# An adaLN transformer block on one core: first MLP weights are split during the first attention block, and the plan counts the queue of transfers

## The chip, the cores and the metric

One core of a Trainium2 chip runs the whole program. The metric is device time in microseconds of one execution; lower is better.

## The reference

One block of a transformer with adaptive layer norm: 2048 rows of 576, 32 heads of 18, an MLP of width 4608, all in float32.

```python
mod = (_silu(c) @ w_mod).reshape(c.shape[0], 6, 1, -1)
sa, ca, ga, sb, cb, gb = (mod[:, i] for i in range(6))
h = layernorm(x) * (1 + ca) + sa
x = x + ga * (softmax(q @ k.T * Dh**-0.5) @ v) @ wo     # q, k, v = h @ wqkv, by head
h = layernorm(x) * (1 + cb) + sb
x = x + gb * (silu(h @ w1) @ w2)
```

## The kernel before

**Blocks.** After a start that makes the keys, values and the first queries, the rows are worked on in four blocks of 512 (`NQB`). A block's attention goes in eight groups of four heads. An *attention step* is one `psa` matmul (scores by query, of which VectorE takes row maxima, `mx`, L966) and one `psb` matmul (scores by key, of which ScalarE takes the exponential, `pt`, L1049); a group has 64 of them, the `psa` stream runs 38 pairs of steps ahead (`LEAD`), and the products with the values (`psv`, L1057) follow. A group's row maxima go through a transpose (`pst`), a copy (`mt`, L990) and a small transfer into the rows of the query tile (`qt<-mt`, L995); the group's first `psb` waits for that transfer.

**What fills TensorE beside attention.** Beside the first block's attention stand the projections that are left (their weights `wqkv` are loaded raw, L768, and split by ScalarE, L773, and GpSimd, L778). Beside a later block's attention stands everything after attention of the block before (`post`): output projection with `wo`, layer norm, and the MLP in 18 pairs of first-layer tiles (`mlp1`) and nine groups of four second-layer tiles (`mlp2`; group i needs four tiles `w2t` of 128x576). The last block's MLP stands alone at the end.

**Weights.** A float32 product is made of three products of rounded parts, so every weight tile is split into a high part and a low part. On first use, beside the second block's attention, each half of a tile of `wo`, `w1` and `w2` is loaded raw (L1104, three buffers `raw`), scaled by a gate on GpSimd for `wo` and `w2` alone (L1107), split by GpSimd (L1110 a cast, L1113 a subtraction), and the finished tile is stored (L1116). Later blocks load the split tile whole (`wload`, the branch for `b` over 0).

**The order.** All engines run in an order that a planner writes. It keeps a time for TensorE and four other queues (ScalarE, VectorE, GpSimd, SP), and a beam search chooses at each point between an attention step, values, and the next item of the fill. SP issues every DMA, in the order in which the planner sees its operations become ready. In the plan a transfer has landed a fixed time after its issue, whatever else is under way:

```python
LAND, LANDW = 2300, 4000
    def issue(self, dur, key, at=0):
        self.push((Op(SP_, dur, self.real and self.real.load(key), (("k", key),), LAND),), 0, max(self.t + 500, at))
```

and an engine takes what became ready first (`heappop`). A half of a weight tile waits in the plan for the half before it to be issued and for the half three places before it to be split.

Of the kernel before, what the change touches and what calls it, by code (L numbers as in the profile page):

```python
# [68 lines left out]
LAND, LANDW = 2300, 4000  # L69
# [24 lines left out]
class Op:  # L94


    __slots__ = ("eng", "dur", "emit", "sets", "lag")

    def __init__(self, eng, dur, emit=None, sets=(), lag=0):
        self.eng, self.dur, self.emit, self.sets, self.lag = eng, dur, emit, sets, lag  # L100
# [11 lines left out]
class Sim:  # L112


    def __init__(self, fill, ends, loads):
# [3 lines left out]
        self.t = self.n = self.w = 0  # L119
# [62 lines left out]

    def set(self, sets, now, lag=0):
        end = now + lag
        for x in sets:
# [115 lines left out]
    def slots(self):  # L301
# [40 lines left out]
        if j == 0:  # L342
            q = sa // 32 + 1
            if q < NQB * NQUAD and sa == load_at(q):
                self.issue(1440, ("Q", q), late)
            n = sa // 8 + 1
            if sa % 8 == 0 and 6 <= n < 4 * NQB * NQUAD:
                self.issue(1280, ("ka", n))
            n = sb // 8 + 1
            if sb % 8 == 0 and n < 4 * NQB * NQUAD:  # L350
                self.issue(1280, ("kb", n))
            if w == 16 and i + 1 < NQB * NQUAD:
                self.issue(400, ("V", i + 1))
# [12 lines left out]
    def issue(self, dur, key, at=0):  # L366

        self.push((Op(SP_, dur, self.real and self.real.load(key), (("k", key),), LAND),), 0, max(self.t + 500, at))
# [35 lines left out]
    def rows(self):  # L404
# [10 lines left out]
        if kind == "m":  # L415
            self.work(110, "full", rel)
            e = self.real.max_b(i) if self.real else (None, None)
            self.push((Op(DVE_, 270, e[0], (slot,)), Op(SP_, ROWS, e[1], (("k", ("mr", i)),), LAND)), 0, self.t + 150)
# [226 lines left out]
def tile_adaln_block(ctx: ExitStack, tc: tile.TileContext, x, wqkv, wo, w1, w2, c, wfirst, wcol, out):  # L645
# [192 lines left out]
    def add_qk(steps, add):  # L838
        def load(i):
# [12 lines left out]
            add(Item(0, lambda: None, chains=((0, (Op(SP_, 10 if i == 1 else 500, begin, (), 0 if i == 1 else 3000), Op(ACT_, 740, hi), Op(GPS_, 1620, lo, (("k", ("w", i)),)))),)))  # L852

        n_mod = 0
        for i, (which, m, pairs) in enumerate(steps):
            for ns in pairs:
# [12 lines left out]
                def ends(box, which=which, m=m, ns=ns, pid=pid, names=names):  # L869
                    for g in range(2):  # L870
# [8 lines left out]
                        def store(g=g, hl=hl):  # L879
# [3 lines left out]
                               Op(SP_, 1800 if which == XM else 900, store, (("k", names[g]),), LAND))  # L883
# [22 lines left out]
    mods = [(m, t) for m in range(2) for t in range(KT)]  # L906
    FILL.append(Item(0, lambda: None, chains=((0, (Op(DVE_, 280, lambda: mod_load(*mods[0]), (("k", ("dg", mods[0])),)),)),)))
# [171 lines left out]

    def open_mlp():  # L1080
# [10 lines left out]
    def weights(make, src, scr, key, gate=None):  # L1091

        box, sets = {}, []
        for half in range(2):
# [23 lines left out]
            chain = [Op(SP_, 430, load, [], LAND)]  # L1118
            if gate is not None:
                chain.append(Op(GPS_, 804, scaled))  # L1120
            chain += [Op(GPS_, 445, high), Op(GPS_, 880, low, [])]
            if half:
                chain[-1].sets.append(("k", key))
                chain.append(Op(SP_, 390, store))
# [12 lines left out]
    def wload(make, src, scr, key, b, gate=None):  # L1137

        if b == 0:
            return (), tuple(weights(make, src, scr, key, gate))  # L1140
        return ((300, (Op(SP_, 390, lambda: nc.sync.dma_start(f(make()), f(scr)), (("k", key),), LANDW),)),), ()
# [6 lines left out]
    def x_op(b, j):  # L1148
        return Op(SP_, 400, lambda: x_load(b, j), (("k", ("x1", b, j)),), LAND)
# [31 lines left out]
    def post(b, add):  # L1181
# [188 lines left out]
        def mlp2(i0, put):  # L1370
            for j in range(NST):
# [16 lines left out]
                after = (Op(SP_, 400, store, (), LAND),) + ((x_op(b + 1, j + 1),) if b + 1 < NQB and j + 1 < NST else ())  # L1388
# [48 lines left out]
    OPEN.fn, OPEN.keys = open_mlp, tuple(sorted(made))  # L1437
# [451 lines left out]
```

## Time and profile before

| | |
|---|---|
| median of 3 runs | 2495.27 us (2494.88 to 2499.73) |
| the profiled execution | 2495.22 us, span 2493.4 us |
| block ends (last copy into `ot`) | 611.6, 1179.5, 1705.5, 2223.2 us |
| TensorE busy, mean granted clock | 2393.6 us, 0.986 |

The page has a busy time for each engine, 40 slices of the span in tenths, the DMA queues, the chain of work that ended last, and the costliest groups of instructions. In a table of windows the columns are the busy time of each engine with its count of instructions, then the granted TensorE clock, the DMA share (mean of 16 DMA engines) and GB/s. In a list of waits the numbers are the total in us, how often, and the longest. In a timeline they are start and duration in us, and in brackets how long the engine sat idle before and what released it. In a list for one tile they are the shortest, median and longest duration in ns, and the first and last start in us. PE is TensorE, DVE VectorE, ACT ScalarE, POOL GpSimd; SPq is the queue of SyncE.

### The profile page before, as it was taken

What the parts mean: (1) busy time and instruction counts of PE and PEld (TensorE: products, weight loads), DVE (VectorE), ACT (ScalarE), POOL (GpSimd) and SP (SyncE); (2) the same over time, 40 slices, a digit from 0 to 9 for tenths busy, and PEclk for the clock granted to TensorE, in tenths of its full rate; (3) what the DMA queues carried; (4) which work ended last, traced back from release to release, by engine and by line L of the source; (5) the groups of instructions that cost most, each with busy time, mean ns of one, the idle gap of its engine ahead of it and who ended that gap; (6) DMA issues with size and microseconds to landing.
All of it is one profiled execution on the core that took longest, in us unless ns stands there. A gap on an engine that the chain in (4) does not pass through costs nothing.

```text
span 2493.4 us, 52598 instructions
## 1 busy us (share of the span) xinstructions
PE 2393.6 (96%) x20528; PEld 1646.3 (66%) x20528; DVE 1784.4 (72%) x3180; ACT 1498.3 (60%) x2712; POOL 578.1 (23%) x729
## 2 busy tenths in 40 slices
PE   5999999998999999989999999999999999999999
PEld 4874545443566666665666667766677667678988
DVE  7877787787867777767877777778877778424333
ACT  5246776665656666656666776666776677652121
POOL 4100000003455565555121111111311111110000
PEclk9999999998999999999999999999999999999999
DMA  7744434435456565556455544544545555426463
GB/s 248 255 154 153 142 110 140 148 115 180 150 182 203 189 208 188 184 188 224 142 170 184 195 151 149 186 147 160 191 155 168 173 180 172 138 105 241 172 219 120
DMA packets 190711, 428.68 MB, mean 172 GB/s; under 512 B 21442, under 2 KB 58722, under 8 KB 190466
## 3 DMA queue, kind: packets, MB, share of 16 engines
q1 hardware_dynamic: 190466, 425.33, 51.0%
q8 instruction: 164, 2.69, 0.5%
q14 instruction: 81, 0.66, 0.1%
HBM read 338.92 MB, written 85.80 MB: 170 GB/s over the span
## 4 chain that ended last, share of the span: by engine, by line
PE 83%; DMA 6%; DVE 4%; POOL 4%; ACT 1%; issue 1%; SPq 1%; ACTq 0%; POOLq 0%; DVEq 0%
PE ps L722 26%; PE psv L1057 17%; PE psa L964 12%; PE ps L716 10%; PE psb L1047 9%; PE psqk L722 3%; DMA raw<-in_w 2%; PE psp L722 2%; DVE mx L966 2%; PE psv L722 2%; DMA raw<-in_wqkv 1%; DMA kt<-kscr 1%; POOL w2t L1113 1%; POOL raw L1107 1%; PE psv L1617 1%
## 5 line engine op out<-in xcount | busy, mean ns | idle before, releaser
L966 DVE TENSOR_REDUCE mx<-psa 128x1 f32<-128x512 f32 x2048 | 1347.3, 687 | 406.8 <-PE psb L1047 197.5
L1049 ACT ACTIVATE pt<-psb 128x512 f32<-128x512 f32 x2048 | 1169.9, 597 | 597.7 <-PE psb L1047 337.2
L1047 PE MATMUL psb<-qt,kt 56*128 56x512 f32 x2048 | 814.6, 428 | 20.8 <-ACT pt L1049 13.8
L964 PE MATMUL psa<-kt,qt 54*128 54x512 f32 x2048 | 769.1, 416 | 11.1 <-DVE mx L966 8.2
L964 PEld LDWEIGHTS psa<-kt,qt 54*128 54x128 f32 x2048 | 362.7, 187 | 235.4 <-DVE mx L966 128.2
L1057 PE MATMUL psv<-pt,vt 128*32 128x512 f32 x4096 | 507.6, 606 | 0.1
L722 PE MATMUL ps<-w2t,g 64*128 64x288 f32 x4992 | 445.7, 301 | 25.2 <-POOL w2t L1110 14.2
L722 PEld LDWEIGHTS ps<-w2t,g 64*128 64x128 f32 x4992 | 396.1, 189 | 100.9 <-issue 43.1
L1047 PEld LDWEIGHTS psb<-qt,kt 56*128 56x128 f32 x2048 | 365.5, 186 | 78.7 <-ACT pt L1049 62.4
L722 PE MATMUL ps<-hh,w1t 64*128 64x512 f32 x2160 | 383.6, 398 | 0.4 <-POOL w1t L1113 0.3
L722 PEld LDWEIGHTS ps<-hh,w1t 64*128 64x128 f32 x2160 | 213.0, 186 | 57.4 <-ACTq L729 12.3
L1355 POOL TENSOR_TENSOR g<-etmp,g 128x512 fp32r<-128x512 f32 x108 | 137.9, 1292 | 451.4 <-ACT g L1351 436.1
L1057 PEld LDWEIGHTS psv<-pt,vt 128*32 128x32 f32 x4096 | 103.8, 109 | 209.7 <-issue 201.1
L1217 POOL TENSOR_TENSOR x<-x,gt 128x288 f32<-128x288 f32 x116 | 92.9, 801 | 542.3 <-ACT gt L1213 530.6
L722 PE MATMUL ps<-hl,w1t 64*128 64x512 f32 x864 | 178.3, 392 | 0.0
L1210 DVE TENSOR_TENSOR x<-ps,x 128x288 f32<-128x288 f32 x184 | 83.7, 455 | 102.1 <-PE ps L716 70.6
L716 PE MATMUL ps<-w2t,g 128*128 128x288 f32 x960 | 130.1, 295 | 1.4 <-ACT g L1351 0.9
L716 PEld LDWEIGHTS ps<-w2t,g 128*128 128x128 f32 x960 | 128.6, 188 | 2.8 <-ACT g L1351 1.2
L1344 ACT ACTIVATE eq<-ps 128x512 f32<-128x512 f32 x36 | 21.5, 598 | 146.4 <-PE ps L716 146.4
L716 PE MATMUL ps<-hh,w1t 128*128 128x512 f32 x360 | 106.9, 390 | 0.5 <-DVE hh L696 0.5
L778 POOL TENSOR_TENSOR wql<-raw,wqh 128x640 fp32r<-128x640 f32 x13 | 20.8, 1599 | 371.1 <-ACT wqh L773 303.4
L722 PEld LDWEIGHTS ps<-hl,w1t 64*128 64x128 f32 x864 | 88.7, 186 | 14.9
(134 smaller groups left out, 2138.5 us busy)
## 6 DMA issues: line engine op xcount, KB each, us to landing
kt<-kscr SPq DMA_DIRECT2D x1024, 108.0 KB
w1t<-w1s SPq DMA_DIRECT2D x108, 640.0 KB
w2t<-w2s SPq DMA_DIRECT2D x108, 576.0 KB
w1s<-w1t SPq DMA_DIRECT2D x36, 640.0 KB
w2s<-w2t SPq DMA_DIRECT2D x36, 576.0 KB
vt<-vscr SPq DMA_DIRECT2D x32, 608.0 KB
qt<-qscr SPq DMA_DIRECT2D x128, 108.0 KB
raw<-in_w SPq DMA_DIRECT2D x72, 160.0 KB
```

The lines of the kernel that those rows point to most:

```text
L716: mm(self.ps[late], lhsT=lhsT, rhs=rhs, start=(i == 0), stop=(i == self.n - 1))
L722: done = mm(self.ps[g], lhsT=lhsT[rows], rhs=rhs[rows], start=(s == 0), stop=(s == 2 * self.n - 1))
L964: mm(ps, lhsT=t["q"][64 * j:64 * j + 54, hp, stt * P:(stt + 1) * P], rhs=t["k", kc, hp][64 * j:64 * j + 54, :], start=True, stop=True)
L966: return lambda: nc.vector.tensor_reduce(t["mx"][:, 2 * j + hp, stt, kc:kc + 1], ps, axis=AX.X, op=ALU.max)
L1047: mm(ps, lhsT=t["kb", kt // 4, hp][64 * e:64 * e + 56, kt % 4 * P:(kt % 4 + 1) * P], rhs=t["q"][64 * e:64 * e + 56, hp, :], start=True, st ...
L1049: return lambda: nc.scalar.activation(t["P"][kt, hp][:, e, :], ps, AF.Exp, scale=SCALE)
L1057: mm(t["ps"][32 * h:32 * h + 32, :], lhsT=t["v"][:, c0:c0 + 32], rhs=t["P"][kt, h // 2][:, h % 2, :], start=(kt == 0), stop=(kt == NKT - 1 ...
L1107: nc.gpsimd.tensor_tensor(d["raw"], d["raw"], gate[:, d["cs"]], op=ALU.mult)
L1113: nc.gpsimd.tensor_tensor(box["w"][:, 0, d["cs"]], d["raw"], f(box["w"][:, 1, d["cs"]]), op=ALU.subtract)
L1210: nc.vector.tensor_add(c["x1", j][:, hs], ps, c["x1", j][:, hs])
L1217: nc.gpsimd.tensor_add(c["x1", j][:, HH:], c["x1", j][:, HH:], box.pop("gt"))
L1355: (nc.vector if last else nc.gpsimd).tensor_tensor(gt[:, 1, :], d["t"], f(gt[:, 0, :]), op=ALU.subtract)
```

## The change

**The first MLP weights.** A new item (`SPLIT`) stands at the very start of the fill of the first block. It runs two chains, for the even and the odd halves of the 36 tiles of `w1`. Each has one raw buffer and one output buffer, and goes round: SP stores the half that this chain split last and loads its next one, GpSimd casts, GpSimd subtracts. When the last halves are stored, two keys are set, for which the opening of the MLP's buffers at the end of the first block now waits too. Beside the second block's attention the tiles of `w1` are then loaded whole, as in the later blocks; `w2` and `wo` are split there as before.

**The plan.** In place of the fixed landing times each transfer has a length in the queue (`MOVE`); transfers follow each other in one queue, and a result is seen some time after. An SP operation with a transfer that follows another operation of its chain, or that waits for a join, is pushed back by `SLACK`, 2500 ns. GpSimd takes, of the operations that are ready, those first that are not marked `late`; the weight splits are.

```diff
-LAND, LANDW = 2300, 4000
+FIRST, SEEN, SLACK = 1000, 500, 2500
+MOVE = {"k": 4 * 608, "q": 4 * 608, "v": 2300, "m": 320, "raw": 645, "w": 1700, "ws": 1480, "x": 780, "qk": 1640, "rawqk": 1280}
...
     def pop(self, e, s):
-        _, _, chain, i = heappop(self.queue[e])
+        q = self.queue[e]
+        if e == GPS_ and len(q) > 1:
+            x = min((x for x in q if x[0] <= s), key=lambda x: (x[2][x[3]].late, x[0], x[1]))
+            q.remove(x)
+            heapify(q)
+            _, _, chain, i = x
+        else:
+            _, _, chain, i = heappop(q)
...
         end += TR
+        land = end
+        if e == SP_ and op.data:
+            land = self.dma = max(min(s + 330, end) + FIRST, self.dma) + op.data
+            land = max(land, end + FIRST) + SEEN
         if op.sets:
-            self.set(op.sets, end, op.lag)
+            self.set(op.sets, end, land)
         if i + 1 < len(chain):
-            self.push(chain, i + 1, end + op.lag)
+            self.push(chain, i + 1, land + (SLACK if chain[i + 1].eng == SP_ and chain[i + 1].data > MOVE["m"] else 0))
...
                 if n + 1 == x[2]:
-                    self.push(x[3], 0, self.keys[x[1]][1])
+                    self.push(x[3], 0, self.keys[x[1]][1] + (SLACK if x[3][0].eng == SP_ else 0))
...
+    def split(n):
+        d = {}
+        def load(k):
+            d["raw"] = wqp.tile([P, 320], F32, name=f"w1raw{n}", bufs=1)
+            nc.sync.dma_start(d["raw"], w1[k // 2][:, k % 2 * 320:k % 2 * 320 + 320])
+        def store(k):
+            nc.sync.dma_start(f(w1s[k // 2][:, :, k % 2 * 320:k % 2 * 320 + 320]), f(d["out"]))
+        def high():
+            d["out"] = wqp.tile([P, 2, 320], F32R, name=f"w1out{n}", bufs=1)
+            nc.gpsimd.tensor_copy(d["out"][:, 1], d["raw"])
+        def low():
+            nc.gpsimd.tensor_tensor(d["out"][:, 0], d["raw"], f(d["out"][:, 1]), op=ALU.subtract)
+        def turn(k):
+            if k >= 2:
+                store(k - 2)
+            if k < 2 * NFT:
+                load(k)
+        chain = []
+        for k in range(n, 2 * NFT, 2):
+            chain += [Op(SP_, 400 if k < 2 else 800, lambda k=k: turn(k), (), MOVE["raw"] if k < 2 else MOVE["raw"] + 740), Op(GPS_, 445, high, late=True), Op(GPS_, 880, low, late=True)]
+        chain.append(Op(SP_, 400, lambda: turn(2 * NFT + n), (("k", ("w1s", n)),), 740))
+        return tuple(chain)
...
-            chain = [Op(SP_, 430, load, [], LAND)]
+            chain = [Op(SP_, 430, load, [], MOVE["raw"])]
...
-        if b == 0:
+        if b == 0 and gate is not None:
             return (), tuple(weights(make, src, scr, key, gate))
...
-    OPEN.fn, OPEN.keys = open_mlp, tuple(sorted(made))
+    SPLIT.chains = (0, split(0)), (4000, split(1))
+    OPEN.fn, OPEN.keys = open_mlp, tuple(sorted(made)) + (("w1s", 0), ("w1s", 1))
```

**Where instructions moved.** SP's queue in the first block, around the row maxima of the third group of heads; before, only keys (`kt`), values and projection tensors stand there:

```order
L948 DMA kt_79<-kscr 54x512 x2
L948 DMA kt_80<-kscr 54x512 x2
L948 DMA kt_81<-kscr 54x512 x2
L948 DMA kt_82<-kscr 54x512 x2
L995 DMA qt<-mt 2x8x128 x2
L948 DMA kt_83<-kscr 54x512 x2
L948 DMA kt_84<-kscr 54x512 x2
```

The same place after the change, where `w1raw` is a raw half and `w1out` a split one:

```order
L962 DMA kt_81<-kscr 54x512 x2
L962 DMA kt_82<-kscr 54x512 x2
L1103 DMA w1s<-w1out_3394 256x1x320
L1100 DMA w1raw_3440<-in_w 128x320
L1009 DMA qt<-mt 2x8x128 x2
L1103 DMA w1s<-w1out_3437 256x1x320
L1100 DMA w1raw_3490<-in_w 128x320
L962 DMA kt_83<-kscr 54x512 x2
L962 DMA kt_84<-kscr 54x512 x2
L1103 DMA w1s<-w1out_3492 256x1x320
L1100 DMA w1raw_3553<-in_w 128x320
```

A store and a load of a half stand between nearly every two chunks of keys, some ten such turns in a group; the 72nd store stands in the eighth group. The first load of a half stands far ahead, in the start, and its two GpSimd operations stand between the first power and the first copy (L1546) of the start's layer norm.

SP's queue at the end of the first block, around the row maxima of the second block's first group, before; `raw<-in_wo` is half a tile of `wo`, `wos` the store of a split one:

```order
L1104 DMA raw<-in_wo 128x288 x2
L948 DMA kt_81<-kscr 54x512 x2
L948 DMA kt_82<-kscr 54x512 x2
L1104 DMA raw<-in_wo 128x288
L1116 DMA wos<-wo_6973 256x1x576
L995 DMA qt<-mt 2x8x128 x2
L1104 DMA raw<-in_wo 128x288
```

and after:

```order
L1148 DMA raw<-in_wo 128x288
L962 DMA kt_81<-kscr 54x512 x2
L962 DMA kt_82<-kscr 54x512 x2
L1148 DMA raw<-in_wo 128x288
L1009 DMA qt<-mt 2x8x128 x2
L1148 DMA raw<-in_wo 128x288
L1160 DMA wos<-wo_7422 256x1x576
L1148 DMA raw<-in_wo 128x288
```

The maxima stood behind seven loads and two stores of `wo` and stand behind three loads and no store now.

TensorE's queue in the second block, at the end of a group's second first-layer pair (`ps<-hh,w1t`) and the start of its second-layer product (`ps<-w2t,g`), before:

```order
L722 MATMUL ps_14633<-hh,w1t 128x512
L722 MATMUL ps_14634<-hh,w1t 128x512
L722 MATMUL ps_14633<-hh,w1t 128x512
L722 MATMUL ps_14634<-hh,w1t 128x512
L1057 MATMUL psv_14786<-pt_2083,vt_2094 32x512 x2
L1057 MATMUL psv_14786<-pt_2084,vt_2094 32x512 x2
L1057 MATMUL psv_14786<-pt_2085,vt_2094 32x512 x2
L1057 MATMUL psv_14786<-pt_2086,vt_2094 32x512 x2
L1064 MATMUL pso<-ident,ov 128x128 x4
L722 MATMUL ps_14819<-w2t,g 128x288
```

and after:

```order
L1061 MATMUL psb<-qt,kt_83 128x512
L978 MATMUL psa<-kt_77,qt 128x512
L1061 MATMUL psb<-qt,kt_84 128x512
L734 MATMUL ps_15024<-hh,w1t 128x512
L734 MATMUL ps_15025<-hh,w1t 128x512
L734 MATMUL ps_15024<-hh,w1t 128x512
L734 MATMUL ps_15025<-hh,w1t 128x512
L978 MATMUL psa<-kt_77,qt 128x512
L1061 MATMUL psb<-qt,kt_84 128x512
L1071 MATMUL psv_14551<-pt_2087,vt_2094 32x512 x2
L1071 MATMUL psv_14551<-pt_2088,vt_2094 32x512 x2
L734 MATMUL ps_15324<-w2t,g 128x288
```

More attention stands there now. From the first matmul of the group's second first-layer pair to the first with `w2t`, the first eight groups of the second block hold 14, 13, 13, 12, 12, 14, 13 and 10 attention steps before, 101 in all, and 16, 15, 21, 16, 12, 22, 23 and 25 after, 150 in all. In the second half of the fourth block's attention these products stand at the same attention steps as before.

More of the change, by code (lines that the diff above doesn't have):

```diff
@@ L1 @@
-from heapq import heappop, heappush
+from heapq import heapify, heappop, heappush
 from contextlib import ExitStack
@@ L364, in slots, with issue @@
         return True
-    def issue(self, dur, key, at=0):
-        self.push((Op(SP_, dur, self.real and self.real.load(key), (("k", key),), LAND),), 0, max(self.t + 500, at))
+    def issue(self, dur, key, what, at=0):
+        self.push((Op(SP_, dur, self.real and self.real.load(key), (("k", key),), MOVE[what]),), 0, max(self.t + 500, at))
     def values(self, n):
@@ L882, in ends @@
                         yield (Op(ACT_, 600, hi), Op(DVE_, 690, lo, (("p", pid, g),)),
[L883 removed]
+                               Op(SP_, 1800 if which == XM else 900, store, (("k", names[g]),), MOVE["qk"]))
                 out = pair_items(lambda it: None, pid, make, GR, MMC, 14, lambda g, i=i: [("w", i)] if i and g[0] == 0 else [], ends)
@@ L1386, in store @@
                     nc.sync.dma_start(out[b * QB + j * P:b * QB + (j + 1) * P, :], c["x1", j])
-                after = (Op(SP_, 400, store, (), LAND),) + ((x_op(b + 1, j + 1),) if b + 1 < NQB and j + 1 < NST else ())
+                after = (Op(SP_, 400, store, (), MOVE["x"]),) + ((x_op(b + 1, j + 1),) if b + 1 < NQB and j + 1 < NST else ())
                 join = (("j", ("out", b, j), 2, after),) if i0 + CH == NFT else ()
```

36 lines of the change are left out of this document (19 added, 17 removed).

## Prediction

> **What bounds the kernel now.** I read the page first, then the busy times block by block, then who TensorE waits for, then the stretches around those waits.
>
> ```profile
> span 2493.4 us, 52598 instructions
> PE 2393.6 (96%) x20528; PEld 1646.3 (66%) x20528; DVE 1784.4 (72%) x3180; ACT 1498.3 (60%) x2712; POOL 578.1 (23%) x729
> PE   5999999998999999989999999999999999999999
> POOL 4100000003455565555121111111311111110000
> PEclk9999999998999999999999999999999999999999
> ```
>
> TensorE is 96% busy, so only its gaps and its clock are to be had. GpSimd works hard in slices 9 to 19 alone. The four blocks of rows end where GpSimd copies a block's last attention columns (`ot`):
>
> ```profile
> L1078 POOL COPY ot<-ot x4: 396/396/397, 611.6 to 2223.2; 128x256 f32<-128x256 f32 x4
> 1179.48 0.40 POOL L1078 COPY ot<-ot 128x256 f32<-128x256 f32 x1
> 1705.48 0.40 POOL L1078 COPY ot<-ot 128x256 f32<-128x256 f32 x1 [0.20 <-DVE ot L1075]
> core 0: us, PE busy (x) PEld busy (x) DVE busy (x) ACT busy (x) POOL busy (x), PEclk, DMA share, GB/s
> 220.50:611.60 391.10, 368.44 (x2369) 179.84 (x2367) 303.14 (x539) 262.59 (x485) 28.54 (x36) 0.96 0.44 142
> 611.60:1179.50 567.90, 535.09 (x4899) 361.11 (x4900) 424.45 (x720) 363.06 (x656) 321.44 (x447) 0.97 0.58 188
> 1179.50:1705.50 526.00, 523.24 (x5086) 360.11 (x5084) 410.76 (x721) 363.31 (x659) 88.21 (x92) 1.00 0.50 169
> ```
>
> So the second block takes 567.9 us and the third, with the same kinds of work and 187 more matmuls, 526.0: 41.9 us more. The waits in the second block and one of them in time (SP, then GpSimd, then TensorE) say why:
>
> ```profile
> PE ps L722 <- POOL w2t L1110: 14.2, 7, 5.0
> PE ps L722 <- POOL w2t L1113: 10.5, 10, 2.7
> PE psT L1259 <- DVE ot L1245: 2.6, 1, 2.6
> 1060.70 0.36 SPq L1104 DMA_DIRECT2D raw<-in_w  x1
> 1066.47 0.79 POOL L1107 TENSOR_TENSOR raw<-raw,gb 128x288 f32<-128x288 f32 x1 [5.31 <-DMA raw<-in_w]
> 1067.80 0.61 PE L722 MATMUL ps<-w2t,g 64*128 64x288 f32 x2 [5.00 <-POOL w2t L1110]
> 1062.00:1067.00 5.00, 0.80 (x13) 0.56 (x9) 0.90 (x2) 1.18 (x3) 0.53 (x1) 0.99 0.80 242
> ```
>
> TensorE stands for second-layer weights that GpSimd is still splitting, and GpSimd stands for their load: issued by 1061.06, landed 5.4 us later at a DMA share of 0.80, where the plan of before counts 2.3. Each such wait also halves the clock. The block has seven half-clock spells; these are the first, the fifth, the sum of all seven, and the wait ahead of the fifth:
>
> ```profile
> 653.90:660.70 6.80, 5.39 (x21) 2.32 (x22) 4.26 (x10) 2.88 (x5) 5.63 (x9) 0.50 0.76 271
> 944.00:947.40 3.40, 3.31 (x24) 3.31 (x26) 1.35 (x2) 1.08 (x2) 3.32 (x6) 0.50 0.80 273
> sum 37.40, PE 29.87 PEld 23.35 DVE 14.51 ACT 11.35 POOL 34.34; mean PE 4.27 PEld 3.34 DVE 2.07 ACT 1.62 POOL 4.91
> 943.22 0.40 PE L722 MATMUL ps<-w2t,g 64*128 64x288 f32 x2 [1.71 <-POOL w2t L1110]
> ```
>
> 37.4 us at 0.50 lose 18.7 us. The first spell (6.8) follows the layernorm wait of 2.6 us and stays; the other 30.6 lose 15.3.
>
> **The change, part by part.** The sum is against the profiled execution, 2495.22 us (span 2493.4 and 1.8 around it), 0.05 off the median of the runs, 2495.27.
>
> A, the waits for w2t in the second block: 14.2 + 10.5 = 24.7 us. Each group of four tiles has lost its eight w1 halves on GpSimd and SP; the loads that are left are planned with 2.5 us of slack each, and TensorE's order now puts 12 to 25 attention steps (one `psa` and one `psb` matmul each) between the start of the group's second first-layer pair and its first w2t matmul, where 10 to 14 stood. That is six more on average, 4 us of TensorE's time by the step's 0.66 us under E, and the 17 waits had 1.5 us on average and 5.0 at most. I take all of it: -24.7. B, their half clock: -15.3. A + B = -40.0, and the 41.9 us between the blocks bounds them from outside.
>
> ```profile
> raw<-in_w SPq DMA_DIRECT2D x72, 160.0 KB
> w1s<-w1t SPq DMA_DIRECT2D x36, 640.0 KB
> L1110 POOL CAST w1t<-raw x72: 442/452/495, 651.5 to 1132.1; 128x320 fp32r<-128x320 f32 x72
> L1113 POOL TENSOR_TENSOR w1t<-raw,w1t x72: 857/875/1190, 652.9 to 1132.6; 128x320 fp32r<-128x320 f32 x72
> 591.43 0.28 DVE L990 CAST mt<-pst 32x128 fp32r<-32x128 f32 x1 [0.52 <-PE pst L985]
> 598.75 1.74 SPq L995 DMA_DIRECT2D qt<-mt  x2
> 602.61 0.76 PE L1047 MATMUL psb<-qt,kt 56*128 56x512 f32 x1 [5.38 <-issue]
> 539.84 1.32 SPq L995 DMA_DIRECT2D qt<-mt  x2
> L1047 PE MATMUL psb<-qt,kt x64: 387/497/792, 543.8 to 595.8; 56*128 56x512 f32 x64
> 301.87 0.70 SPq L768 DMA_DIRECT2D raw<-in_wqkv  x1
> 307.74 0.74 ACT L773 ACTIVATE wqh<-raw 128x640 fp32r<-128x640 f32 x1 [2.17 <-DMA raw<-in_wqkv]
> 24.87 0.24 POOL L1546 COPY xt<-xt 128x64 f32<-128x64 f32 x1 [2.57 <-ACT xt L1543]
> 1074.43 1.07 PE L1057 MATMUL psv<-pt,vt 128*32 128x512 f32 x8
> PE psa L964 <- DVE mx L966: 1.5, 5, 0.5
> ```
>
> C, the end of the first block: the row maxima are ready at 591.7, but their transfer starts at 598.75, behind the split and store of wo on SP's queue, and `psb` waits 5.4 us. In the new order the maxima stand ahead of the first wos store, and wo's loads are apart. I take -5.4, between that and 0 if the wait only moves.
>
> D, the splits in the first block. GpSimd: 72 x (0.45 + 0.88) = 96 us, on an engine that is busy 28.5 of 391 us there: hidden; the few weight splits it does for the projection can stand behind one, with a lead of tens of us. The pair that stands in the start lies ahead of this 24.87 copy, in a gap of 2.57 us: 1.3 us fit, cost 0, about 1 if its load is late. SP: 144 more issues of about 0.4, 58 us on a queue that mostly waits for TensorE. Transfers: 72 x (160 + 320) KB = 35.4 MB over 391 us, 90 GB/s on 142, so the DMA share goes from 0.44 to about 0.72. Who is late next? The loads of keys are issued a chunk (16 steps) ahead; the row maxima are not: issued by 541.16, used at 543.8, 2.6 us later with no spare. At the loaded 5.4 us (share 0.80) against this 2.6, each boundary could lose 2.8 us; at 0.72, 0.28/0.36 of that, 2.2. Of seven boundaries inside the block I take three as tight: +6.5; the bounds are 0 and 7 x 2.8 = 20. ScalarE's wait at 307.74 for the projection weights (5.2 us after their issue) is of the same kind: with five of these between -5 (the plan now foresees them) and +5, I take 0.
>
> E, the attention steps that fill the w2 waits: counted over the eight groups, 49 more stand there. Such a step, with nothing beside it, takes 52.0/64 = 0.81 us (the 543.8 to 595.8 row) and TensorE needs about 0.39 (the row's shortest) + 1.07/4 for its values = 0.66 of it: 49 x 0.15 = +7 at most, 0 if the fill rides along. I take +4.
>
> F, all else: planned transfers in the third block on are a little closer, and its order differs slightly; the longest total wait of TensorE in the third block was 1.5 us (the last row above), for VectorE: 0, within 3 either way.
>
> Sum: -40.0 - 5.4 + 6.5 + 4 = -34.9, so 2495.2 - 34.9 = **2460 us**.
>
> Two rules against this sum. At 944 a wait of 1.71 us is followed by 3.4 us at half clock. The Trainium skill (TensorE: Matmul & The Clock Gate, Part 1) has the clock fall after an idle window of about 3.4 us; by that only the 5.00 us wait would have cost clock, B would be 3.4 and the time 2472 as an estimate, and the trace does not agree with it. For D, the Trainium skill (DMA: Bandwidth & Descriptors, Latency and other measured facts) gives HBM access 0.2 us on average and 2 at high load; by it all seven boundaries lose 1.8, D is 12.6 and the time 2466, an estimate too; the 5.4 us landing agrees in direction.
>
> **The rivals.**
>
> W2 still late. The new plan spaces the raw loads by its slack, and GpSimd puts other ready work first; where the real landing is still later than planned, half of A and B stays: 2460 + 20 = 2480. For it: 5.4 us landings at a share of 0.80; against it: in this block 72 + 36 transfers of w1 become 36, and 72 x 160 KB are gone. 16%.
>
> The attention loads lose (slower). Each turn on SP stores the half split two turns ago and loads the next; SP is in order, so a turn whose split is not done holds every key, query and maxima load behind it. In the new order some ten turns stand in the attention of four heads, 55 us by the row below, so each of the two chains has 11 us per turn and needs 5.4 (landing) + 1.3 (split) + the issues: 3 us are spare. From the point where landing passes about 9 us, every further us is paid up to 72 times: at 1.0 us over, 2460 + 72 = 2532. For it: SP, the transfers and GpSimd all sit in one chain; against it: 5.4 is already a loaded landing, and a load of keys has 16 steps, some 13 us, of cover. 6%.
>
> ```profile
> L1047 PE MATMUL psb<-qt,kt x65: 387/493/504, 211.3 to 266.7; 56*128 56x512 f32 x65
> ```
>
> No net gain. The waits go, but the second block is then held by VectorE and ScalarE where attention was moved in, and by late maxima in the first: E 7, D 20, and C's wait stays: -40 + 27 = -13; with a third of A and B left as well, 2495. For it: attention alone runs at 0.81 a step; against it: the third block runs at 526 with the same work. 8%.
>
> Full gain. C and A + B in full, 41.9 + 5.4, D and E near 0: 2448. 12%.
>
> **How the numbers follow.** The forecast has 58%. The range is that of the forecast (D 0 to 20, E 0 to 7, C 0 to -5.4, F 3) stretched to the full gain and to half-late w2: 2443 to 2486. About 0.2%, 5 us, is what a measurement of this kernel can tell from no change. Faster: 58 + 16 + 12, and 3 of the no-gain case, 89%; same 5%; slower 6%.
>
> **What would show it.** Right: the stretch between the first two `ot` copies falls from 567.9 to about 530 at a clock of 1.00, w2t leaves the list of waits, GpSimd falls from 321 to about 226 us there and rises from 28.5 to about 124 in the first block, whose length stays within 8 us of before. C: no wait of 5 us ahead of the block's last `psb`. Wrong: w2t waits over 8 us, or a first block more than 15 us longer with `psb` waiting for `qt` or `kt`.

## The result and the profile after

| | before | after |
|---|---|---|
| median (range), 4 runs each on one chip | 2496.07 us (2494.88 to 2499.73) | 2466.81 us (2463.68 to 2469.76) |
| ratio, 95% interval | | 0.988 [0.9863, 0.9897] |
| profiled execution, its span | 2495.22, 2493.4 us | 2466.89, 2465.1 us |
| ends of the blocks | 611.6, 1179.5, 1705.5, 2223.2 | 601.7, 1153.2, 1676.4, 2194.9 |

The kernel became faster, by 28.3 us between the two profiled executions; 34.9 were forecast. First the page of the kernel after: busy times and GpSimd's slices.

```profile
span 2465.1 us, 52723 instructions
PE 2391.9 (97%) x20528; PEld 1632.2 (66%) x20528; DVE 1777.0 (72%) x3180; ACT 1491.2 (60%) x2712; POOL 581.9 (24%) x729
POOL 4213332303333434344311111111211111110000
```

The copies that end the blocks, and the table of windows between them:

```profile
L1092 POOL COPY ot<-ot x4: 389/397/398, 601.7 to 2194.9; 128x256 f32<-128x256 f32 x4
...
1153.23 0.39 POOL L1092 COPY ot<-ot 128x256 f32<-128x256 f32 x1
...
1676.42 0.40 POOL L1092 COPY ot<-ot 128x256 f32<-128x256 f32 x1 [0.19 <-DVE ot L1089]
...
223.00:601.70 378.70, 366.31 (x2375) 178.78 (x2372) 306.37 (x541) 263.52 (x488) 100.53 (x145) 0.96 0.70 223
601.70:1153.20 551.50, 537.20 (x4934) 350.35 (x4934) 419.87 (x730) 364.65 (x666) 225.86 (x298) 0.99 0.52 170
1153.20:1676.40 523.20, 518.94 (x5033) 357.28 (x5033) 404.68 (x708) 354.76 (x646) 99.55 (x107) 1.00 0.52 173
1676.40:2194.90 518.50, 516.66 (x5010) 357.82 (x5009) 361.24 (x642) 359.35 (x660) 88.42 (x91) 1.00 0.47 161
```

GpSimd's work moved as the prediction had it: 225.86 us in the second block (226 said) and a DMA share of 0.70 in the first (0.72 said). (In the first block it is busy 100.53 us, where about 124 were said; 12 of the 72 splits stand ahead of 223.) But two signs of being right did not come. The second block is 551.5 us long, not 530. The first ends 9.9 us earlier, though it carries most of the new transfers, and between the edges of the two tables it is 12.4 us shorter (378.70 for 391.10), where its length was to stay within 8 us. The waits of the second block after, and its two half-clock spells:

```profile
POOL raw L1151 <- DMA raw<-in_w: 91.6, 31, 8.8
PEld psa L978 <- DVE mx L980: 48.4, 83, 1.5
PE psa L978 <- DVE mx L980: 7.2, 18, 0.7
PE ps L734 <- POOL w2t L1157: 0.9, 2, 0.6
```

```profile
880.60:884.00 3.40, 3.40 (x20) 1.59 (x17) 1.28 (x5) 0.77 (x2) 0.71 (x1) 0.50 0.78 307
1054.70:1058.10 3.40, 3.30 (x19) 2.58 (x19) 3.00 (x6) 2.80 (x7) 2.19 (x4) 0.50 0.72 262
```

The same waits in the second block of the kernel before:

```profile
POOL raw L1107 <- DMA raw<-in_w: 33.3, 21, 5.3
POOL w1t L1110 <- DMA raw<-in_w: 21.0, 22, 3.8
PEld psa L964 <- DVE mx L966: 23.0, 37, 1.3
```

So TensorE no longer stands for `w2t`: 0.9 us where 24.7 stood, and 6.8 us at half clock where 37.4 stood. In their place two other numbers have grown: GpSimd waits 91.6 us for raw loads, where it waited 54.3 (33.3 for w2, 21.0 for w1) with twice as many halves to split, and TensorE's weight loads for `psa` wait twice as long for VectorE's row maximum (48.4 us for 23.0).

The 6.8 us are not what is left of the seven spells of before. The wait of the layer norm, which was to keep its 6.8 us at half clock, is 1.68 us long now and has none behind it:

```profile
645.54 0.66 PE L1303 MATMUL psT<-ident,ot 128*128 128x128 f32 x4 [1.68 <-DVE ot L1289]
...
645.60:649.00 3.40, 3.40 (x25) 2.44 (x25) 2.19 (x5) 3.09 (x6) 2.01 (x3) 1.00 0.56 170
```

The two spells of after have no wait of 1 us ahead of them. Each begins inside a run of attention steps with no dense matmul between them, one of 5 steps (875.5 to 882.2) and one of 10 (1047.4 to 1055.5).

At the end of the first block, the row maxima of the next group in the timeline after:

```profile
586.03 0.28 DVE L1004 CAST mt<-pst 32x128 fp32r<-32x128 f32 x1 [1.50 <-PE pst L999]
586.34 1.33 SPq L1009 DMA_DIRECT2D qt<-mt  x2
...
593.05 0.46 PE L1061 MATMUL psb<-qt,kt 56*128 56x512 f32 x1
```

Their transfer starts 0.03 us after they are ready, 7.0 us after it before, and the matmul that uses them has no wait in brackets.

A second wait of the first block has shrunk. ScalarE stands for the projection weights that it splits, before (first line) and after:

```profile
ACT wqh L773 <- DMA raw<-in_wqkv: 13.8, 6, 3.6
...
ACT wqh L785 <- DMA raw<-in_wqkv: 4.6, 2, 4.0
```

The exponentials stand behind these splits on ScalarE, and TensorE's waits for them fall from 10.4 to 7.1 us in the block.

### The profile page after: what moved, and what is told of

It reads as the page before. It is cut to its first block, busy times and chain, and to the rows that moved or that the text cites. A ratio compares the mean times of both kernels' runs of the same rounds, so it can differ in the third digit from the quotient of the medians.

```text
span 2465.1 us, 52723 instructions
## 1 busy us (share of the span) xinstructions
PE 2391.9 (97%) x20528; PEld 1632.2 (66%) x20528; DVE 1777.0 (72%) x3180; ACT 1491.2 (60%) x2712; POOL 581.9 (24%) x729
## 4 chain that ended last, share of the span: by engine, by line
PE 88%; DMA 4%; DVE 4%; ACT 1%; POOL 1%; issue 1%; SPq 0%; ACTq 0%; POOLq 0%; DVEq 0%
PE ps L734 28%; PE psv L1071 18%; PE psa L978 12%; PE ps L728 10%; PE psb L1061 9%; PE psqk L734 4%; DVE mx L980 2%; PE psp L734 2%; PE psv L734 1%; PE pso L1078 1%; DMA kt<-kscr 1%; PE psp L728 1%; DMA w1raw<-in_w 1%; ACT pt L1063 1%; DMA xt<-in_x 1%
## 5 line engine op out<-in xcount | busy, mean ns | idle before, releaser
L1071 PE MATMUL psv<-pt,vt 128*32 128x512 f32 x4096 | 514.4, 608 | 0.3
L734 PEld LDWEIGHTS ps<-w2t,g 64*128 64x128 f32 x4992 | 384.9, 185 | 75.1 <-issue 41.9
L734 PE MATMUL ps<-w2t,g 64*128 64x288 f32 x4992 | 427.1, 297 | 2.4 <-DVE x L1254 1.2
L1391 DVE SCALAR_TENSOR_TENSOR etmp<-etmp 128x512 f32<-128x512 f32 x108 | 73.1, 710 | 15.9 <-ACT etmp L1388 15.9
```

What stands on the lines that cost most here:

```text
L734: done = mm(self.ps[g], lhsT=lhsT[rows], rhs=rhs[rows], start=(s == 0), stop=(s == 2 * self.n - 1))
L1071: mm(t["ps"][32 * h:32 * h + 32, :], lhsT=t["v"][:, c0:c0 + 32], rhs=t["P"][kt, h // 2][:, h % 2, :], start=(kt == 0), stop=(kt == NKT - 1 ...
L1391: nc.vector.scalar_tensor_tensor(d["t"], d["t"], 1.0, d["u"], op0=ALU.add, op1=ALU.mult)
```

## The experiments

The change has four parts that can be taken apart: the model of transfers (`FIRST`, `SEEN`, `MOVE`), the slack of 2.5 us, GpSimd's new order (`late`), and the split of w1 beside the first block. Twelve kernels were run. In the table below a part is named where the kernel has it; "block" is the length of the second one, "first" the end of the first. "Steps" are the second block's attention steps in TensorE's queue, and of these the ones in runs of 4 or more, with no dense matmul between them. Ratios are to the kernel before on the same chip.

| kernel | time, us | ratio [95%] | first | block | steps, in runs |
|---|---|---|---|---|---|
| before | 2496.07 | | 611.6 | 567.9 | 510, 36 |
| late order | 2475.14 | 0.9911 [0.9894, 0.9928] | 611.9 | 545.2 | 510, 40 |
| model | 2448.70 | 0.9816 [0.9794, 0.9839] | 595.0 | 542.1 | 521, 49 |
| model, late | 2443.78 | 0.9795 [0.9777, 0.9813] | 595.1 | 534.2 | 521, 48 |
| model, late, slack | 2532.71 | 1.0148 [1.0129, 1.0168] | 602.2 | 618.4 | 521, 75 |
| split | 2542.06 | 1.0189 [1.0173, 1.0205] | 675.2 | 550.8 | 510, 32 |
| model, late, split | 2450.04 | 0.9821 [0.9805, 0.9837] | 606.1 | 530.3 | 512, 44 |
| the same, slack in first block | 2447.29 | 0.9815 [0.979, 0.9839] | 595.0 | 527.9 | 507, 48 |
| the same, slack from second on | 2466.33 | 0.9881 [0.9861, 0.9901] | 609.2 | 548.4 | 523, 68 |
| after (all four) | 2466.81 | 0.988 [0.9863, 0.9897] | 601.7 | 551.5 | 519, 84 |
| all four, slack 5 us | 2565.34 | 1.028 [1.0262, 1.0298] | 602.1 | 620.1 | 516, 74 |
| all four, w2 early | 2458.34 | 0.9851 [0.9836, 0.9867] | 602.7 | 542.1 | 522, 81 |
| model, late, split, w2 early | 2447.56 | 0.9811 [0.9794, 0.9828] | 608.5 | 523.8 | 510, 36 |
| model, late, w2 early | 2456.82 | 0.9842 [0.9822, 0.9863] | 598.2 | 552.9 | 523, 90 |

A block's length is that of one execution, the profiled one; that was the slowest of its kernel for the plan without the split (2539.21 us) and for model, late, w2 early (2460.77), and the fastest for slack in the first block alone (2438.24). The order of TensorE's work in the first block is the same after and with slack in the first block alone, yet one ended it at 601.7 and the other at 595.0: the first had 13.7 us at half clock from 573.4 on, the second none there. Differences of 7 us between single blocks decide nothing.

**The plan without the split.**

```diff
-    SPLIT = Item(0, None)
-    FILL.append(SPLIT)
...
-        if b == 0 and gate is not None:
+        if b == 0:
```

> The new model of transfers with no split of w1 in the first block: the 72 halves are split beside the second block, as before. Theory 1, the two parts share the gain (the plan brings the first block, the absent w1 work brings the second): the first block ends near 602 as in the changed kernel, the second block, with GpSimd at about 320 us again, takes 558 to 566 against 551.5, and the time is about 2475 to 2481. Theory 2, the plan alone is the gain and the splits beside the first block bring nothing: 2462 to 2470. Theory 3, the splits and stores cost in the first block, as term D had it, and the plan pays for them there: the first block ends at 595 or earlier.

It took 2532.71 us, slower than before: none of the three theories had that. The first block ends at 602.2, within a microsecond of the kernel after, so there the splits cost nothing measurable beside a plan with slack. The second block is 50 us longer than before, and its waits say for what:

```profile
PE ps L734 <- POOL w2t L1152: 18.1, 9, 3.7
PE ps L734 <- POOL w1t L1152: 9.3, 3, 3.7
PE ps L734 <- POOL w2t L1155: 3.5, 7, 1.7
PE ps L734 <- POOL w1t L1155: 2.4, 3, 1.6
...
602.20:1220.60 618.40, 569.04 (x4938) 370.17 (x4938) 421.62 (x732) 367.49 (x668) 316.83 (x441) 0.95 0.53 172
```

33.3 us stand for weights, more than before the change, at a mean DMA share of 0.53 against 0.58: the share gives no sign that the transfers were the limit.

**The split without the plan.**

```diff
-        q = self.queue[e]
-        if e == GPS_ and len(q) > 1:
...
+        _, _, chain, i = heappop(self.queue[e])
...
-            land = self.dma = max(min(s + 330, end) + FIRST, self.dma) + op.data
-            land = max(land, end + FIRST) + SEEN
+            land = end + {MOVE["w"]: 4000, MOVE["rawqk"]: 3000}.get(op.data, 2300)
...
-FIRST, SEEN, SLACK = 1000, 500, 2500
+FIRST, SEEN, SLACK = 1000, 500, 0
```

> The split of w1 beside the first block, with the planner of before: fixed landings of 2300, 3000 and 4000 ns, no slack, GpSimd in plain order. Theory 1, the parts share the gain: the first block ends at 612 to 618 (the loads of wo still stand ahead of the maxima, and D is small), the waits for w2t in the second block fall from 24.7 to some 8 to 12 us because its transfers and GpSimd are lighter, that block takes about 540 to 550, and the time is 2470 to 2482. Theory 2, the plan alone is the gain: the w2t waits stay near 24 us and the time is 2490 or more. Theory 3, D costs some 20 us where the plan doesn't know of the splits: first block 625 or later.

The second block is the 540 to 550 of theory 1 (550.8), the first ends 63.6 us later than before, three times the 20 us of theory 3. Its two largest waits of TensorE up to 675.2, and the largest wait of ScalarE for a transfer in the first block:

```profile
PE psb L1053 <- ACT pt L1055: 43.3, 17, 15.4
PE psb L1053 <- DMA kt<-kscr: 20.6, 4, 17.0
...
ACT wqh L777 <- DMA raw<-in_wqkv: 61.9, 7, 17.9
```

Two stretches in time, the first with SP, GpSimd, ScalarE and TensorE, the second with ScalarE and TensorE:

```profile
205.86 0.52 SPq L1095 DMA_DIRECT2D w1s<-w1out  x1
...
218.40 0.70 SPq L772 DMA_DIRECT2D raw<-in_wqkv  x1
219.15 2.58 SPq L954 DMA_DIRECT2D kt<-kscr  x4
...
204.43 0.45 POOL L1099 CAST w1out<-w1raw 128x320 fp32r<-128x320 f32 x1 [6.58 <-DMA w1raw<-in_w]
...
225.70 0.74 ACT L777 ACTIVATE wqh<-raw 128x640 fp32r<-128x640 f32 x1 [17.92 <-DMA raw<-in_wqkv]
226.98 1.28 PE L1053 MATMUL psb<-qt,kt 56*128 56x512 f32 x2 [17.05 <-DMA kt<-kscr]
...
361.42 0.74 ACT L777 ACTIVATE wqh<-raw 128x640 fp32r<-128x640 f32 x1 [16.34 <-DMA raw<-in_wqkv]
362.69 1.28 PE L1053 MATMUL psb<-qt,kt 56*128 56x512 f32 x2 [15.44 <-ACT pt L1055]
```

SP's turns stand ahead of the other loads. GpSimd stands 6.58 us for a raw half, and the stores stand for GpSimd. Behind them in SP's queue stands a load of projection weights, which goes out at 218.40, when ScalarE has already stood for it since 207.8. ScalarE stands 17.92 us in all, the exponentials are behind it in ScalarE's order, and TensorE stands for them. The profile puts TensorE's 17.05 us down to the keys, and keys issued at 219.15 may have landed no earlier. But the four largest waits of TensorE in this block (17.05, 7.77, 15.44 and 11.14 us) all end 1.3 us after ScalarE took up such a split again, behind a wait of 8.2 to 17.9 us. So late projection weights explain all four, and the keys by themselves are not shown to cost more than a few us. This is the rival "the attention loads lose" of the prediction in that SP's turns hold other loads back, with the old plan in place of the new; what was held where it hurt was the projection weights.

**No slack.**

```diff
-FIRST, SEEN, SLACK = 1000, 500, 2500
+FIRST, SEEN, SLACK = 1000, 500, 0
```

> The changed kernel with the planner's slack of 2.5 us ahead of large loads set to 0: loads go out as soon as the model lets them, and in the second block the longest bunch of attention steps that stands within the second layer falls from 11 to 6. Theory 1, what kept the second block at 551.5 in place of about 532 is attention that stands in bunches, where TensorE goes at VectorE's pace: with shorter bunches that block takes 540 to 547 and the time is 2455 to 2463. Rival, the slack is what keeps w2t off the path: the waits for w2t come back with 8 to 15 us and the time is 2472 to 2482.

2450.04 us, better than theory 1 had it; the second block is 530.3, the wait for `w2t` there 0.5 us. The slack was not needed to keep `w2t` off the path, and cost 17 us. It shows in the traces as lateness of the loads. From the split that frees a raw buffer to the issue of the load that goes into it, 10.6 us pass on average in this kernel, 12.6 in the kernel after and 16.0 with a slack of 5 us (82 loads each). In the two kernels without the split of w1 (154 loads) the median is 0.4 us without slack and 3.7 with it.

**W2 asked for one pair earlier, with the slack.**

```diff
-                mlp1(i0 + 2, [(NG // 2, i0 + 1)])
-                mlp1(i0 + CH, [(0, i0 + 2), (0, i0 + 3)])
+                mlp1(i0 + 2, [(0, i0 + 1), (NG // 2, i0 + 2), (NG // 2, i0 + 3)])
+                mlp1(i0 + CH)
```

> The changed kernel with the w2 loads of each group asked for one pair of first-layer tiles earlier. The order now has 243 attention steps inside the second layer of that block, against 222, in 137 places against 129, with runs up to 14 against 11. Theory 1, the price lies in how long the bunches of attention are and not in when w2 lands: no gain, 2464 to 2474. Rival, w2 is still the late one and the plan fills with attention only because of it: second block 535 to 543, time 2450 to 2458.

2458.34 us and 542.1: the block lies in the rival's range, the time 0.3 us above it. Theory 1, that only the runs of attention count, failed as stated: with 81 steps in runs against 84 the block gained 9 us, of which 3.3 are half clock that the kernel after had there and this one had not.

**Slack in the first block alone.**

```diff
+            self.push(chain, i + 1, land + (SLACK if not self.block and chain[i + 1].eng == SP_ and chain[i + 1].data > MOVE["m"] else 0))
...
+                    self.push(x[3], 0, self.keys[x[1]][1] + (SLACK if not self.block and x[3][0].eng == SP_ else 0))
```

> The changed kernel with the planner's slack of 2.5 us kept in the first block alone. In the second block 48 attention steps then stand in runs of 4 or more (no dense matmul between them), where the changed kernel has 84 and the run without any slack 44. Theory 1, the slack costs through these runs and only in the second block, and is worth some 4 us in the first (601.7 against 606.1 without it): first block ends near 602, second block 528 to 534, time 2443 to 2450. Rival, the gain of the run without slack comes from the start or the first block and reaches the second through where that begins: second block 540 or more, time 2455 to 2465.

2447.29 us (2438.24 to 2456.49, a wide spread), in theory 1's range; the block of the fastest execution is 527.9, its first block ends at 595.0 and not near 602. The second block's row of the windows, and two of its waits:

```profile
595.00:1122.90 527.90, 518.67 (x4892) 349.10 (x4892) 412.83 (x717) 358.52 (x654) 234.81 (x314) 1.00 0.55 180
...
POOL raw L1151 <- DMA raw<-in_w: 36.6, 16, 8.6
PEld psa L978 <- DVE mx L980: 30.4, 50, 1.1
```

With the same splits in the block, GpSimd stands 36.6 us for raw loads, not 91.6; without any slack it was 55.9.

**Slack from the second block on alone.** The same two places, the other way round:

```diff
+            self.push(chain, i + 1, land + (SLACK if self.block and chain[i + 1].eng == SP_ and chain[i + 1].data > MOVE["m"] else 0))
...
+                    self.push(x[3], 0, self.keys[x[1]][1] + (SLACK if self.block and x[3][0].eng == SP_ else 0))
```

> The changed kernel with the slack of 2.5 us from the second block on alone, the other half of the run that keeps it in the first block alone (2447.3). 68 steps of the second block stand in runs of 4 or more. Theory 1, the slack does its harm in the second block, and the first block is some 4 to 11 us longer without it: first block 604 to 608, second 542 to 552, time 2462 to 2472. Rival, the harm needs the first block's slack: second block 535 or less, time 2450 to 2457.

2466.33 us, block 548.4, first block 609.2: theory 1. The harm of the slack lies in the second block, where GpSimd's wait for raw loads is 79.3 us again. The first block without slack ends later in both runs with the split (606.1 and 609.2, against 595.0 and 601.7 with it). But half clock has cost 13.7 and 23.9 us up to there in the first two and 8.5 and 17.1 in the others, so how much of that is the slack stays open.

**Slack doubled.**

```diff
-FIRST, SEEN, SLACK = 1000, 500, 2500
+FIRST, SEEN, SLACK = 1000, 500, 5000
```

> The changed kernel with a slack of 5 us in place of 2.5. 74 steps of the second block stand in runs of 4 or more, against 84. Theory 1, slack costs through the runs: second block 544 to 552, time 2460 to 2468. Rival, slack costs by its own length, some 21 us for each 2.5 (530.3 without it, 551.5 with it), since each turn of the raw buffers is longer by it: second block 568 to 576, time 2483 to 2492.

2565.34 us, block 620.1: worse than either theory. GpSimd's wait for raw loads hardly grows; TensorE now waits itself. Second block:

```profile
POOL raw L1151 <- DMA raw<-in_w: 94.7, 30, 8.8
PE ps L734 <- POOL w2t L1154: 32.0, 17, 4.3
PE ps L734 <- POOL w2t L1157: 4.7, 13, 0.5
```

These waits, 36.7 us where the kernel after has 0.9, and 72.9 us at half clock where it has 6.8, which cost 33 us more, make up the 68.6 us by which the block is longer. Why the plan put no more attention in front of them stays open.

**Neither slack nor split.** The edit of the plan without the split, and:

```diff
-FIRST, SEEN, SLACK = 1000, 500, 2500
+FIRST, SEEN, SLACK = 1000, 500, 0
```

> The model of transfers without slack and without the split beside the first block. With slack this took 2532.7 and its second block 618.4, 50 more than before, with 33 us of waits for w1t and w2t. Theory 1, the slack is what made it slow: each raw buffer is asked for 2.5 us later per turn, and 108 turns on GpSimd don't fit: the second block falls to 555 to 570, w1t leaves the list of waits, and the time is 2480 to 2492. Rival, the model of transfers itself is what is slow with 108 splits in the block (GpSimd serves its late ones last): second block 600 or more, time 2515 or more.

2443.78 us, far below theory 1's range and the fastest of the study. The splits of the second block fit, with no wait for w1t or w2t: the slack alone had made them late, some 89 us of it. (They are 154 halves and not the 108 of the expectation: 72 of `w1`, 72 of `w2` and 10 of `wo`.) Against the run with the split and no slack (2450.04) the two intervals overlap a little; so the split beside the first block brings nothing here, and may cost 6 us.

**No slack, w2 early.** The change of all four parts with both edits:

```diff
-FIRST, SEEN, SLACK = 1000, 500, 2500
+FIRST, SEEN, SLACK = 1000, 500, 0
...
-                mlp1(i0 + CH, [(0, i0 + 2), (0, i0 + 3)])
+                mlp1(i0 + CH)
```

> No slack, and the w2 loads asked for one pair earlier. 36 steps of the second block stand in runs of 4 or more, as in the kernel before. Theory 1, the runs of attention are what is left: second block 524 to 530, time 2443 to 2450. Rival, after the slack is gone the floor is the dense work and the attention in it, and neither runs nor w2 matter: as without slack, 2448 to 2453.

2447.56 us. The block is the shortest of all (523.8, with the 36 steps in runs of before), but the time is not told apart from the other kernels without slack.

**The model alone, and GpSimd's order alone**, both without split and slack. The first:

```diff
-        if e == GPS_ and len(q) > 1:
...
+        _, _, chain, i = heappop(self.queue[e])
```

> The kernel before with the model of transfers alone: no split beside the first block, no slack, and GpSimd in plain order, not with its weight splits last. With GpSimd's new order this took 2443.8. Theory 1, the modelled landings are the gain, GpSimd's order nothing: 2441 to 2450, second block 530 to 538. Rival, GpSimd's order is what takes the weight splits off the path of the rest: 2465 or more.

The second keeps GpSimd's selection and has the fixed landings:

```diff
-            land = self.dma = max(min(s + 330, end) + FIRST, self.dma) + op.data
-            land = max(land, end + FIRST) + SEEN
+            land = end + {MOVE["w"]: 4000, MOVE["rawqk"]: 3000}.get(op.data, 2300)
```

> The kernel before with GpSimd's new order alone: fixed landings of 2300, 3000 and 4000 ns, no slack, no split beside the first block. Theory 1, the modelled landings are the gain: 2488 to 2500, second block 562 to 572, waits for w2t of 20 us or more. Rival, GpSimd's order is the gain: 2445 to 2470.

2448.70 us for the model, as theory 1 said. But GpSimd's order alone takes 2475.14, which is in neither range, 21 us off where theory 1 had nothing: waits for `w2t` of 8.5 us in place of 24.7. Each part helps alone; on top of the model the order is worth 5 us, not told apart from none. Why the order by itself shortens those waits stays open.

**Without slack and split, w2 early.** Neither slack nor split, as above, and:

```diff
-                mlp1(i0 + 2, [(NG // 2, i0 + 1)])
-                mlp1(i0 + CH, [(0, i0 + 2), (0, i0 + 3)])
+                mlp1(i0 + 2, [(0, i0 + 1), (NG // 2, i0 + 2), (NG // 2, i0 + 3)])
+                mlp1(i0 + CH)
```

> The model of transfers without slack and without the split beside the first block, and the w2 loads asked for one pair earlier: in the second block 90 attention steps stand in runs of 4 or more, where 48 stood at 2443.8 us, 523 steps against 521 in all. Theory 1, such runs are dear by themselves, because VectorE takes 0.69 us for the maximum of each step: second block 542 to 550, time 2451 to 2460. Rival, the runs in the changed kernel only go along with late loads, and cost nothing where no load is late: second block 530 to 537, time 2440 to 2447.

2456.82 us, 13.0 more, and a block of 552.9 against 534.2: theory 1, the block 2.9 us over its range. Without slack, with no wait for weights, TensorE's runs of attention are dear by themselves:

```profile
PEld psa L976 <- DVE mx L978: 52.5, 95, 1.5
598.20:1151.10 552.90, 540.60 (x4948) 350.63 (x4948) 427.90 (x733) 368.18 (x669) 318.05 (x444) 0.98 0.58 192
```

The price of a run can be read in the kernel after. The windows of four of its runs in the second block, of 11, 9, 10 and 9 steps, and VectorE in the second of them:

```profile
809.20:818.40 9.20, 7.74 (x52) 2.81 (x52) 6.97 (x16) 5.20 (x10) 2.88 (x6) 1.00 0.75 255
988.70:994.60 5.90, 4.93 (x28) 1.91 (x26) 5.17 (x9) 4.57 (x9) 2.31 (x5) 1.00 0.44 123
1047.50:1055.50 8.00, 6.76 (x39) 2.58 (x37) 6.44 (x14) 5.18 (x10) 4.05 (x7) 0.95 0.52 144
1107.90:1114.70 6.80, 5.69 (x34) 2.10 (x36) 5.65 (x12) 5.00 (x9) 5.11 (x9) 1.00 0.49 158
sum 29.90, PE 25.11 PEld 9.39 DVE 24.23 ACT 19.94 POOL 14.35; mean PE 6.28 PEld 2.35 DVE 6.06 ACT 4.99 POOL 3.59
...
988.28 2.66 DVE L980 TENSOR_REDUCE mx<-psa 128x1 f32<-128x512 f32 x4
991.67 3.84 DVE L980 TENSOR_REDUCE mx<-psa 128x1 f32<-128x512 f32 x6 [0.73 <-PE psb L1061]
```

In a run TensorE can go no faster than VectorE's maxima, here one per 0.64 to 0.67 us. These four runs hold 39 steps and 69 `psv` matmuls, 24.4 us at 0.39 and 1.07/8 each, and took 29.9: TensorE stood idle 4.8 us in them. VectorE was not busy throughout either (24.23 of 29.9 us): while TensorE does values it gets no new scores, as in the 0.73 us ahead of 991.67, so the two stand for each other by turns. Waits of TensorE's weight loads for the maximum grow with the steps in runs, 30.4 us with 48, 48.4 with 84 and 52.5 with 90.

Over the table a step more in a run goes with some 0.2 to 0.4 us: from model and late to the same with w2 early, 18.7 us, of which 8.5 are 17 us at half clock and 1.3 two more steps, leave 8.9 for 42 steps; from no slack to the kernel after, 21.2 less 1.7 of clock and 4.6 for seven more steps leave 14.9 for 40. The four windows show 0.14 us a step (29.9 less 24.4, by 39). So not all of it is lost inside the long runs; where the rest is lost is not shown.

## Why the prediction was right, and where its steps were not

The direction and the range held, and of the mechanism the part that the waits for w2t and their half clock would go. Why they went was another matter, and the sum came within 6.6 us partly by luck: it holds two larger errors of opposite sign.

| step | forecast | measured or left over |
|---|---|---|
| A, waits for w2t | -24.7 | 0.9 left: -23.8 |
| B, their half clock | -15.3 | 37.4 to 6.8 us: -15.3 |
| E, attention moved into the w2 waits | +4 (0 to 7) | +20.7 |
| C and D, first block | -5.4 + 6.5 = +1.1 | -9.9 |
| F, the rest | 0 | in the above |
| sum | -34.9 | -28.3 |

E's +20.7 is not measured by itself but is what A and B don't explain: the second block fell by 16.4 where they give 39.1, the third by 2.8, and the fourth grew by 0.8.

**A** was right to 0.9 us. **B** has the right size partly by luck: it kept the 6.8 us of the first spell, behind the layer norm's wait, and let the others go. All seven went, the first too, and two new ones of 3.4 us came in runs of attention. Waits of 1.43 to 1.71 us for `w2t` did have half clock behind them before, but the layer norm's 1.68 us after did not: a wait of under 2 us can cost the clock and need not.

**E failed: "49 x 0.15 = +7 at most, 0 if the fill rides along. I take +4."** Two things were left out. The 49 steps were counted in one place of each group, not where they came from: the second block does nine more attention steps in all (519 for 510), about 6 us by the same 0.66, of which the third block's 13 fewer gave back only 2.8. And the price was set on those 49 alone, while the runs stand in the whole block, 84 steps where 36 stood.

**Under E lies the slack**, which the prediction counted as safety ("the loads that are left are planned with 2.5 us of slack each"). It is a delay: a load that is planned 2.5 us later stands later in SP's queue, GpSimd waits for it, the plan knows that `w2t` will be late, and fills with attention until it comes (the lateness and the runs are measured; that the plan ties the one to the other is read from its code). In this kernel the waits for `w2t` vanish from the trace because they have been filled, not because the weights come early. Without slack, 530.3 us: the "about 530" of the forecast, in a kernel that keeps all the rest.

**C** was right: the wait of 5 us is gone. **D had the wrong sign as a sum for this kernel.** "Of seven boundaries inside the block I take three as tight": in the kernel after no wait of 1 us for row maxima stands inside the block, and what the prediction set to 0 there, ScalarE's waits for projection weights, brought a gain. The waits of TensorE that went about account for the 9.9 us: C 5.4, for exponentials 3.3, for keys 1.3; half clock costs 17.1 us up to the block's end both before and after. Without slack the block does end 11.0 us later with the split (595.1 to 606.1), within D's bounds, but 3.5 of that are half clock, and the waits behind it are ScalarE's for projection weights (2.6 to 10.6 us) more than late maxima (one of 1.3 us); with slack nothing shows (602.2 to 601.7). And the plan's own gain in the first block was put at C alone: model and late, with neither slack nor split, end it at 595.1, 16.5 us earlier than before, 11 more than C; 6.9 of them are half clock.

**The rivals.** "W2 still late" fell: no w2t wait over 0.6 us in the second block. "The attention loads lose" was given 6% for the change as it is, and did not come, but turns of the split do hold other loads: with the old plan the first block ends 63.6 us later. What stood for its load there was above all ScalarE, whose projection weights the prediction's cover of 16 steps for keys does not touch. The new plan, with its modelled landings and GpSimd's order, prevents it even without slack (606.1). "No net gain" named two of the right causes, VectorE in the second block and the first block's maxima; only the first came.

What the split was for was not asked in the prediction, and is the larger surprise: the gain is the plan's. Model and order alone take 2443.78, the split adds nothing to it, and its worth in the changed kernel, from 2532.71 to 2466.81, is, as far as these runs tell, that with fewer loads in the second block fewer are delayed by the slack: without slack that worth is gone (2443.78 to 2450.04).

## What to carry to other kernels

Where a planner fills waits, a wait that leaves the list may have become work placed in front of it: count how that work stands, in runs or between other work, and price a run by its slowest engine, here VectorE, as a lower bound. Where an engine waits for several things, look at what their makers wait for: the largest waits of the split alone read as keys and exponentials, and lay behind a late load for ScalarE. A margin in a plan's times is a delay of the real transfer when the plan also fixes the queue's order; try it at zero before moving work to pay for it. When a change has several parts, price each alone and against the others: here two halves of the change were each slower than before, and one part alone, without its margin, beat the whole.

## What was not expected of the hardware

The clock can fall after short waits, as before the change. In the plan without the split, TensorE's matmul after a wait of 1.57 us, and the window behind it:

```profile
896.94 0.79 PE L734 MATMUL ps<-hh,w1t 64*128 64x512 f32 x1 [1.57 <-POOL w1t L1155]
...
897.00:900.40 3.40, 3.40 (x16) 3.20 (x18) 0.69 (x1) 0.60 (x1) 3.26 (x5) 0.50 0.22 61
```

Half-clock spells also come without such a wait: 13.7 us from 573.4 on in the kernel after, where no gap of TensorE in the first block past 416.3 exceeds 0.8 us, and none at the same place in another execution of the same order. What sets these off stays open; by their size, 3 to 7 us of the time each, they set how well two single executions can be compared.
